# A never-taken branch behind another wait, a residual as one matrix product, and the order of the store's two waits, in a one-core decode kernel

## The chip, the cores and the metric

The kernel runs on one core of a Trainium2 chip. A core has five engines that run their own instruction streams and meet only through semaphores: TensorE (PE in the profile; PEld is its weight loads), VectorE (DVE), ScalarE (ACT), GpSimd (POOL) and SyncE (SP), which issues the transfers. Sixteen DMA engines carry data between the device memory and the on-chip memory. The metric is the device time of one execution in microseconds. For the kernel before, three runs gave 190.36, 190.53 and 191.09 us, so the median is 190.53 us.

## What is computed

One token goes through an attention block over a long cache and then through a small MLP block. Cut to what matters:

```python
def _A_ref(x, k_cache, v_cache, wq, wo):           # 32 query heads, 8 cached heads, 16384 positions
    q = (x @ wq) as heads of 128
    p = softmax(q . k * 128 ** -0.5)
    return (p . v) @ wo

def _B_ref(x, w1, w2, w3, w4):                     # S = 1
    h  = gelu(layernorm(x) @ w1)
    hs = shifted(h) @ w2                           # shifts along a sequence of length 1
    x1 = x + hs
    return x1 + gelu(layernorm(x1) @ w3) @ w4      # w3: 512 x 1792, w4: 1792 x 512

h  = x + _A_ref(layernorm(x), ...)
h2 = h + _B_ref(layernorm(h), ...)
```

For one position the four shifted quarters of `h` are all zero, so `hs` is zero and `w1` and `w2` have no part in the output; the kernel doesn't load them. What is left of the second block is two normalizations, the product with w3, gelu, the product with w4 and the residual sums.

## The kernel before

The weights and the cache are read once, some 79 MB, by SyncE's transfers in the order of the program: wq, then keys and values of four pairs of cached heads, then wo in three pieces (`WO`), w3 in two (`W3`) and w4 in four (`W4`, cut at rows 5, 10 and 13 of 14 steps). Keys go alternately into two halves of `kb`, values into `vb`; wo later takes the first half of `kb`, and w3 and w4 take the second. A transfer into a buffer waits until its readers are done.

TensorE runs the four pairs in a loop with register waits (`_tensor`, lines 154 to 316): scores from transposed keys (L600), softmax pieces, the product with the values (L636), a gather (L658). Behind the loop stands straight-line code, which is what the change is about: the product with wo (L702), a sum over rows (L708), the statistics of the normalization (L493), the product with w3 (L720), the residual (L738) and the product with w4 (L746).

The layout of the tail: the 512 outputs stand as four blocks of 128 columns in four groups of 32 partitions of the bank `n_ps`. `BLOCK = (0, 2, 1, 3)` says which block stands in which group. The residual L738 is four products, one per group; each takes 32 columns of the fp32 identity `ident_f` as weights and `xsum` (128x128, fp32) as the moving matrix, and opens the accumulation. L746 adds to it, in 14 steps `m` of four products each. Step `m` needs the piece of w4 that holds its rows and the half of `hcol` that holds its column: steps 0 to 6 need `("hcol", 0)`, steps 7 to 13 `("hcol", 1)`. `hcol` is the transposed gelu: ScalarE makes gelu in two halves `hg` (L729), VectorE transposes each (L733).

A recording layer, `Program`, keeps for each engine the list of operations with the operations they depend on. `_wants` turns these into one wait per semaphore, and `_run` puts the waits ahead of the instruction, unless an earlier wait of the same engine covered them. An operation whose function is `None` marks the place of a branch: on TensorE `pe(None)` (L744) stands ahead of step `W4[-2][0]`, which is 10; on VectorE `dve(None)` (L736) stands behind the transposes. There `_tensor` and `_vector` emit a comparison that is never true, with a jump back to early code and a hint for it:

```python
self._run(eng, ops[hi:on], seen)
eng.br_lt(rl, 0, "pe_pair", "pe_on").branch_hint(hint)
nc.switch_bb("pe_on", parent=None)
self._run(eng, ops[on + 1:], seen)
```

What the marker depends on is not looked at: L314 emits no wait of its own.

At the end ScalarE (L751) and VectorE (L753) copy a half each of the result into `fin`, and SyncE stores it (L754), waiting for both, then waits for the store (L756). The first of its two waits in the program is carried by the store itself, the other by an instruction of its own ahead of it.

GpSimd makes the identity at the start (L520), fills `qb` and `pt` with zeros (L534, L535), computes two small powers (L509) and tells TensorE that values have landed.

Of the kernel before, what the change touches and what calls it, by code (L numbers as in the profile page):

```python
# [6 lines left out]
FP32 = mybir.dt.float32  # L7
# [17 lines left out]
class Program:  # L25
# [128 lines left out]
    def _tensor(self):  # L154
        nc, eng, ops = self.nc, self.nc.tensor, self.ops["PE"]
# [40 lines left out]
        for o in loop:  # L196
            a = o.at
            v = waits.get((a[0], last, *a[2:]))
# [14 lines left out]
        sem, v0, _ = told[0, 0]  # L213
# [4 lines left out]
        r, rl, ry, rq, rk = (eng.alloc_register(n) for n in ("seen", "landed", "half", "query", "piece"))  # L218
# [3 lines left out]
        seen = {}  # L222
# [87 lines left out]
        seen[id(sem)] = told[last, parts - 1][2]  # L310
        on = next(n for n, o in enumerate(ops) if o.fn is None)
        self._run(eng, ops[hi:on], seen)

        eng.br_lt(rl, 0, "pe_pair", "pe_on").branch_hint(hint)  # L314
        nc.switch_bb("pe_on", parent=None)
        self._run(eng, ops[on + 1:], seen)
# [15 lines left out]
W4 = ((0, 5), (5, 10), (10, 13), (13, 14))  # L332
BLOCK = (0, 2, 1, 3)
# [9 lines left out]
def bass_sequential_preLN__gqa_block_cached__mixer_s_mlp__decode_kernel(  # L343
# [13 lines left out]
    with ExitStack() as ctx:  # L357
        sb = lambda name, shape, dt: ctx.enter_context(nc.sbuf_tensor(name, shape, dt))
# [13 lines left out]


        x4 = sb("x4", [4, 128], BF16)
        mean4 = sb("mean4", [128, 128], FP32)
        ident_f = sb("ident_f", [128, 128], FP32)
        ident = sb("ident", [4, 4], BF16)
# [34 lines left out]
        xsum = sb("xsum", [128, 128], FP32)  # L412
        hg = sb("hg", [128, FQ], BF16)
        hT = sb("hT", [128, NCH, 32], FP32)
        hcol = sb("hcol", [128, NHC, 32], BF16)
        fin = sb("fin", [64, 256], BF16)
# [13 lines left out]
        m_ps, n_ps = mn_ps[:, 0:256], mn_ps[:, 256:512]  # L430
# [28 lines left out]
        def dve(fn, r=(), w=(), bank=()):  # L459
            return P.op("DVE", fn, r, w, bank)  # L460
# [4 lines left out]
        def pool(fn, r=(), w=(), bank=()):  # L465
            return P.op("POOL", fn, r, w, bank)

        def pe(fn, r=(), w=(), bank=(), also=()):

            return P.op("PE", fn, r, w, bank, also=also)  # L470

        def piece(cuts, m):
            return [lo <= m < hi for lo, hi in cuts].index(True)
# [23 lines left out]
        def variance(i):  # L497
# [7 lines left out]
            for n in range(1 + i):  # L505
# [22 lines left out]
            r=["ident", "x4"], w=["quarter"])  # L528
        pe(lambda e: e.matmul(O_ps[0][:, 0:128], quarter[:, :, :].rearrange("p q u -> p (q u)"), x4[:, :],
                              start=True, stop=True), r=["quarter"], w=[("O", 0)], bank=[("O", 0)])  # L530
# [2 lines left out]
        act(lambda e: e.activation(scr[0:1, 0:1], mean4[0:1, 0:1], ACTF.Exp), r=["mean4"], w=["scr"])  # L533
        pool(lambda e: e.memset(qb[:, :, :, :], 0.0), w=["qb"])  # L534
        pool(lambda e: e.memset(pt[:, :, :, :, :], 0.0), w=["pt"])  # L535

        dve(lambda e: e.tensor_reduce(row32[:, :], ident_f[:, :].rearrange("p (c r) -> p r c", c=4), AX.X, ALU.add),
            r=["ident_f"], w=["row32"])
        dve(lambda e: e.tensor_reduce(maskdd[:, :], ident_f[:, :].rearrange("p (n d) -> p d n", d=4), AX.X, ALU.add),
            r=["ident_f"], w=["maskdd"])  # L540
# [6 lines left out]
        for z, m, key, mk in ((zo, rowgh, "zo", "rowgh"), (zd, maskgh, "zd", "maskgh")):  # L547
# [5 lines left out]
            r=["hT", (("st", 0), 0), (("st", 0), 6)] + [("v", x) for x in range(VP)], w=["xn"])  # L553
# [3 lines left out]
        for i, key in enumerate(keys):  # L557
            P.part("query", i)
            for k in range(NCH):
                pe(lambda e, k=k: e.matmul(row[:, bass.ds(P.b, 512)], copies(xn[:, k:k + 1], 128),  # L560
                                           wq_k[:, k, bass.ds(P.c, REP * DH)], start=(k == 0), stop=(k == NCH - 1)),
                   r=["xn"], also=[("v", x) for x in range(VP)], w=["n" if key == "mn" else key], bank=[key])
        P.part()
        for g in range(2):
            half = banks[64 * g:64 * g + 64, PAIRS * g:PAIRS * g + PAIRS, :].rearrange("p j c -> p (j c)")
            for b in range(2):
# [3 lines left out]
                    r=["n" if x == "mn" else x for x in keys[PAIRS * g:PAIRS * g + PAIRS]], w=["qcol"],  # L570
                    bank=keys[PAIRS * g:PAIRS * g + PAIRS])
# [120 lines left out]
        for n, (lo, hi) in enumerate(W4):  # L692
# [4 lines left out]
            r=["o_m"], w=["o_f"])  # L697
        dve(lambda e: e.tensor_copy(o_b[:, :], o_f[:, :]), r=["o_f"], w=["o_b"])

        for r_ in range(32):  # L700
# [3 lines left out]
               r=["o_b", ("r", 0, piece(WO, r_))], w=[("O", 0)], bank=[("O", 0)])  # L704
        h_ps, hkey = banks[:, 6, :], "spare0"
        dve(lambda e: e.tensor_copy(osum[:, :], O_ps[0][:, :]), r=[("O", 0)], w=["osum"], bank=[("O", 0)])  # L706
        for q in range(4):
            pe(lambda e, q=q: e.matmul(h_ps[32 * q:32 * q + 32, 0:128], copies(row32[:, 0:1], 32),  # L708
                                       osum[:, q * 128:(q + 1) * 128], start=True, stop=True),
               r=["osum", "row32"], w=[hkey], bank=[hkey])  # L710
        s = st[1]
# [3 lines left out]
            r=["hT", (S, 0)] + [("r", 1, 0)], w=["hc"])  # L715


        for k in range(NCH):
            for q in range(4):
                pe(lambda e, k=k, q=q: e.matmul(s_ps[32 * q:32 * q + 32, 0, 0:FQ], hc[:, k, :],  # L720
                                                w3_sb[:, k, q * FQ:(q + 1) * FQ], start=(k == 0), stop=(k == NCH - 1)),
                   r=["hc"] + [("r", 1, n) for n in (piece(W3, k),) if n], w=[("s", 0)], bank=[("s", 0)])
# [3 lines left out]
            r=["hr", "xs", (S, 6)], w=["xsum"])  # L726
# [7 lines left out]
                hcol[:, lo:hi, :].rearrange("p m u -> p (m u)"),  # L734
                hg[:, :].rearrange("p (i m) -> p m i", m=NHC)[:, lo:hi, :]), r=[("hg", n)], w=[("hcol", n)])
        dve(None)  # L736
        for o in range(4):
            pe(lambda e, o=o: e.matmul(  # L738
                n_ps[32 * o:32 * o + 32, 0:128], ident_f[:, 32 * BLOCK[o]:32 * BLOCK[o] + 32], xsum[:, :],
                start=True, stop=False, skip_group_check=True),  # L740
               r=["ident_f", "xsum"], w=["n"], bank=["mn"])
        for m in range(NHC):
            if m == W4[-2][0]:
                pe(None)  # L744
            for o in range(4):
                pe(lambda e, m=m, o=o: e.matmul(  # L746
                    n_ps[32 * o:32 * o + 32, 0:128], hcol[:, m, :], w4_sb[:, m, BLOCK[o] * 128:(BLOCK[o] + 1) * 128],
                    start=False, stop=(m == NHC - 1),
                    skip_group_check=True),
                   r=[("hcol", 2 * m // NHC), ("r", 1, len(W3) + piece(W4, m))], w=["n"], bank=["mn"])  # L750
        act(lambda e: e.activation(fin[:, 0:128], n_ps[0:64, 0:128], ACTF.Identity),  # L751
            r=["n"], w=[("fin", 0)], bank=["mn"])
        dve(lambda e: e.tensor_copy(fin[:, 128:256], n_ps[64:128, 0:128]), r=["n"], w=[("fin", 1)])  # L753
        P.op("SP", lambda e: e.dma_start(out[0, 0:1, :].rearrange("o (q j) -> (o q) j", q=2), fin[31:33, :]),  # L754
             r=[("fin", 0), ("fin", 1)], w=["out"], dma="out")
        P.op("SP", lambda e: e.nop(), r=["out"])  # L756
        P.emit()

# [29 lines left out]
```

## Time and profile before

| what | value |
|---|---|
| median of three runs | 190.53 us |
| the profiled execution's own time | 190.37 us |
| its span, first to last instruction | 188.84 us |
| mean granted TensorE clock | 0.82 |
| read from device memory | 79.17 MB, 419 GB/s over the span |
| busy: PE, DVE, ACT, POOL | 62%, 61%, 5%, 3% |
| store issued, span ends | 187.69 us, 188.84 us |

The profile is of one execution. Times in it are microseconds from the start of the span, and L12 is line 12 of the kernel. The time of a run is longer than the span, since it also has what stands ahead of the first and behind the last instruction. A row of the timeline merges neighbouring instructions of a kind: start, length, engine, line, operation, output<-inputs, shapes, their count, and in brackets how long the engine had been idle before it and what released it. A "q" behind an engine's name means its sequencer: waits, branches and the issue of transfers. The chain of waits follows the work that ended last back from the end, at each step to what released it.

### The profile page before, as it was taken

Reading aid. Unit: us, or ns where it says so; the run is one execution under the profiler, and the core shown is the slowest. Engines: PE = TensorE matmul, PEld = TensorE weight load, DVE = VectorE, ACT = ScalarE, POOL = GpSimd, SP = SyncE. Lnnn points to the kernel's source line nnn. Section 1 sums busy time; section 2 is a strip of 40 time slices with the busy share of each in tenths; the row PEclk is TensorE's granted clock in tenths of the full one; section 3 lists DMA queues with packets and bytes.
Section 4 is the critical chain, followed back from the end, with each engine's and each line's share of the span. In section 5 each row is a group of like instructions: output and inputs, shape, how many; then the busy total and the mean of one; then the engine's idle time right before and its main releaser. Section 6 shows DMA issues by size and latency. Waiting matters only on the chain.

```text
span 188.8 us, 2175 instructions
## 1 busy us (share of the span) xinstructions
PE 116.5 (62%) x701; PEld 45.5 (24%) x701; DVE 115.4 (61%) x140; ACT 9.3 (5%) x16; POOL 5.7 (3%) x10
## 2 busy tenths in 40 slices
PE   1009908998174499950732999616739996192754
PEld 1003303433031134320310333202213332030222
DVE  4900599995524999945047989550279897514052
ACT  3000000000200000002000000020000000500011
POOL 1900000000000000000000000000000000000010
PEclk9999965999759669996596699965766999669685
DMA  6999999999799999898999999999999999989994
GB/s 222 444 444 444 444 423 465 444 444 444 333 444 444 444 555 416 389 430 347 423 437 444 444 444 444 444 444 396 403 423 444 444 444 444 430 380 423 415 408 168
DMA packets 3325, 79.19 MB, mean 419 GB/s; under 512 B 378, under 2 KB 508, under 8 KB 1276
## 3 DMA queue, kind: packets, MB, share of 16 engines
q1 hardware_dynamic: 3316, 79.17, 97.8%
q8 instruction: 1, 0.02, 0.0%
q10 hardware_dynamic: 8, 0.00, 0.0%
HBM read 79.17 MB, written 0.00 MB: 419 GB/s over the span
## 4 chain that ended last, share of the span: by engine, by line
DMA 66%; DVE 17%; PE 9%; issue 6%; SPq 1%; DVEq 0%
DMA kb<-in_A_k_cache_dram 45%; DVE kt L583 15%; DMA kb<-in_B_w_dram 14%; DMA vb<-in_A_wq_dram 7%; PE banks L560 5%; PE banks L600 4%; SPq L434 1%; DVE qcol L567 1%; DVE qb L574 0%; PE banks L746 0%; PE banks L594 0%; DVE xn L551 0%; DVE fin L753 0%; SPq L137 0%; DVEq L137 0%
## 5 line engine op out<-in xcount | busy, mean ns | idle before, releaser
L583 DVE STREAM_TRANSPOSE kt<-kb 128x2048 int32<-128x2048 int32 (+1 forms) x37 | 71.3, 1989 | 5.6 <-DMA kb<-in_A_k_cache_dram 4.0
L600 PE MATMUL banks<-kt,qn 128*128 x256 | 69.4, 416 | 0.4
L600 PEld LDWEIGHTS banks<-kt,qn 128*128 x256 | 26.3, 103 | 41.9 <-issue 26.2
L636 PE MATMUL banks<-vb,pt 128*32 128x512 bf16 x256 | 21.3, 505 | 2.9 <-POOLq L449 2.9
L652 DVE TENSOR_SCALAR od<-banks,rowc 128x128 f32<-128x128 f32 x4 | 1.4, 350 | 23.3 <-PE banks L636 23.3
L560 PE MATMUL banks<-vb,xn 128*128 x32 | 9.4, 467 | 9.8 <-DVE xn L551 9.8
L594 PE MATMUL banks<-qn 128*128 128x512 bf16 x8 | 4.0, 496 | 18.1 <-DVE kt L583 17.8
L625 DVE STREAM_TRANSPOSE pt<-p_sb 64x1024 bf16<-64x1024 bf16 x8 | 9.9, 1239 | 5.4 <-ACT p_sb L621 5.3
L621 ACT ACTIVATE p_sb<-banks,bias 128x1024 bf16<-128x1024 f32 x4 | 4.5, 1114 | 155.5 <-DVE nmh L617 155.5
L643 PE MATMUL banks<-acc,zd 128*32 128x1 f32 x8 | 1.1, 202 | 17.7 <-DVE pt L625 17.7
L636 PEld LDWEIGHTS banks<-vb,pt 128*32 128x32 bf16 x256 | 8.0, 123 | 14.3 <-issue 8.5
L610 DVE TENSOR_REDUCE mx<-banks 128x1 f32<-128x1024 f32 x4 | 4.9, 1224 | 8.1 <-PE banks L600 8.1
L567 DVE STREAM_TRANSPOSE qcol<-banks 64x1024 f32<-64x1024 f32 x4 | 4.8, 1227 | 7.5 <-PE banks L560 7.5
L560 PEld LDWEIGHTS banks<-vb,xn 128*128 128x128 bf16 x32 | 3.7, 116 | 15.1 <-issue 12.8
L509 POOL TENSOR_TENSOR st<-st,expo 128x1 f32<-128x1 f32 (+1 forms) x2 | 1.3, 630 | 176.2 <-DVE st L507 176.2
L613 PE MATMUL banks<-mxd,mean 128*128 128x128 f32 x8 | 2.0, 326 | 6.6 <-DVE mxd L611 6.6
L594 PEld LDWEIGHTS banks<-qn 128*128 128x128 bf16 x8 | 0.8, 100 | 20.9 <-issue 20.8
L658 PE MATMUL banks<-od,zo 128*32 128x128 f32 x8 | 1.6, 285 | 6.5 <-DVE od L655 6.5
L702 PE MATMUL banks<-kb,o_b 128*32 128x512 bf16 x32 | 3.5, 621 | 2.8 <-DMA kb<-in_A_wo_dram 2.8
L643 PEld LDWEIGHTS banks<-acc,zd 128*32 128x32 f32 x8 | 0.7, 140 | 18.4 <-DVE pt L625 18.4
L655 DVE SCALAR_TENSOR_TENSOR od<-banks,rowc,od 128x128 f32<-128x128 f32 x12 | 4.2, 351 | 0.4
L706 DVE COPY osum<-banks 128x512 f32<-128x512 f32 x1 | 0.7, 692 | 5.3 <-PE banks L702 5.3
(71 smaller groups left out, 45.2 us busy)
## 6 DMA issues: line engine op xcount, KB each, us to landing
kb<-in_A_k_cache_dram SPq DMA_DIRECT2D x8, 4096.0 KB, 29.7
vb<-in_A_v_cache_dram SPq DMA_DIRECT2D x2, 4096.0 KB, 29.0
vb<-in_A_wq_dram SPq DMA_DIRECT2D x1, 4096.0 KB, 12.3
kb<-in_A_wo_dram SPq DMA_DIRECT2D x1, 3072.0 KB, 27.4
kb<-in_B_w_dram SPq DMA_DIRECT2D x1, 1344.0 KB, 23.3
kb<-in_B_w_dram SPq DMA_DIRECT2D x2, 640.0 KB, 25.7
kb<-in_A_wo_dram SPq DMA_DIRECT2D x1, 768.0 KB, 28.9
kb<-in_B_w_dram SPq DMA_DIRECT2D x1, 448.0 KB, 24.1
```

Source lines behind the costliest of these rows:

```text
L560: pe(lambda e, k=k: e.matmul(row[:, bass.ds(P.b, 512)], copies(xn[:, k:k + 1], 128), wq_k[:, k, bass.ds(P.c, REP * DH)], start=(k == 0), s ...
L567: dve(lambda e, g=g, b=b, half=half: e.transpose(qcol[64 * g:64 * g + 64, 2 * b:2 * b + 2, :, :].rearrange("p e m u -> p (e m u)"), half.r ...
L583: P.op("DVE", lambda e, view=view: e.transpose(view(kt), view(kb[y])), r=[("r", y, i) for i in range(RPARTS)], w=[("kt", t + i) for i in r ...
L594: pe(lambda e: e.matmul(row[:, bass.ds(P.y, 512)], copies(none, 128), copies(none, 512), start=True, stop=False, skip_group_check=True), r ...
L600: pe(lambda e, n=n: e.matmul(row[:, bass.ds(P.y, 512)], qn[:, n, bass.ds(P.q, 128)], key_piece(P.k, n), start=False, stop=(n == 3), skip_g ...
L610: dve(lambda e: e.tensor_reduce(mx[:, :], s_all, AX.X, ALU.max), r=[("s", 0), ("s", 1)], w=["mx"], **both)
L613: pe(lambda e: e.matmul(m_ps[:, 0:128], mean4[:, :], mxd[:, :], start=True, stop=True), r=["mxd", "mean4"], w=["m"], bank=["mn"])
L621: act(lambda e: e.activation(p_sb[:, :], s_all, ACTF.Exp, bias=bias[:, 0:1], scale=float(SCALE), accum_out=acc[:, :]), r=[("s", 0), ("s", ...
L625: dve(lambda e, g=g: e.transpose(pt[64 * g:64 * g + 64, :, :, g, :], p_sb[64 * g:64 * g + 64, :]), r=["p"], w=["pt"])
L636: pe(lambda e, l=l, ct=ct, ch=ch: e.matmul(O_ps[0][32 * ct:32 * ct + 32, :], pt[:, l, ch, :, :].rearrange("p g u -> p (g u)"), tiles[:, l ...
L655: dve(lambda e, block=block, c=c: e.scalar_tensor_tensor(od[:, :], block, rowc[:, c:c + 1], od[:, :], ALU.mult, ALU.add), r=[key, "rowc", ...
L702: pe(lambda e, r_=r_, q=q: e.matmul(O_ps[0][32 * q:32 * q + 32, :], copies(o_b[:, r_:r_ + 1], 32), wo_sb[:, r_ * D:(r_ + 1) * D], start=(r ...
```

## The change

It has three edits.

1. The marker `pe(None)` moves from step 10 (`W4[-2][0]`) to step 5 (`W4[0][1]`) and now reads `("hcol", 1)`; `_tensor` emits the waits of the marker ahead of the branch and notes them, so that step 7 needs no wait for the same half any more.
2. The four residual products with 32 columns of the identity each become one product with a 128x128 matrix `swapped`: the identity with its two middle blocks of 32 columns exchanged. GpSimd makes it once at the start, behind the two fills. `swapped` is a new tile of 512 bytes per partition, allocated behind `x4`.
3. The store names the half from VectorE ahead of the one from ScalarE, so that the wait it carries itself is the one for VectorE.

```diff
@@ -310,7 +310,10 @@
         on = next(n for n, o in enumerate(ops) if o.fn is None)
         self._run(eng, ops[hi:on], seen)
-
+        for i, (s, v, _) in self._wants(ops[on]).items():
+            if seen.get(i, 0) < v:
+                eng.wait_ge(s, v)
+                seen[i] = v
         eng.br_lt(rl, 0, "pe_pair", "pe_on").branch_hint(hint)
...
         x4 = sb("x4", [4, 128], BF16)
+        swapped = sb("swapped", [128, 128], FP32)
...
         pool(lambda e: e.memset(pt[:, :, :, :, :], 0.0), w=["pt"])
+        pool(lambda e: e.tensor_copy(swapped[:, :].rearrange("p (b a c) -> p b a c", a=2, b=2),
+                                     ident_f[:, :].rearrange("p (a b c) -> p b a c", a=2, b=2)),
+             r=["ident_f"], w=["swapped"])
...
         dve(None)
-        for o in range(4):
-            pe(lambda e, o=o: e.matmul(
-                n_ps[32 * o:32 * o + 32, 0:128], ident_f[:, 32 * BLOCK[o]:32 * BLOCK[o] + 32], xsum[:, :],
-                start=True, stop=False, skip_group_check=True),
-               r=["ident_f", "xsum"], w=["n"], bank=["mn"])
+        pe(lambda e: e.matmul(
+            n_ps[:, 0:128], swapped[:, :], xsum[:, :], start=True, stop=False, skip_group_check=True),
+           r=["swapped", "xsum"], w=["n"], bank=["mn"])
         for m in range(NHC):
-            if m == W4[-2][0]:
-                pe(None)
+            if m == W4[0][1]:
+                pe(None, r=[("hcol", 1)])
...
         P.op("SP", lambda e: e.dma_start(out[0, 0:1, :].rearrange("o (q j) -> (o q) j", q=2), fin[31:33, :]),
-             r=[("fin", 0), ("fin", 1)], w=["out"], dma="out")
+             r=[("fin", 1), ("fin", 0)], w=["out"], dma="out")
```

On TensorE the program of the tail is then: one residual product, the 20 products of steps 0 to 4, the wait for the second half of `hcol` with the branch, the 36 products of steps 5 to 13, each w4 piece still waited for at its first step. VectorE, ScalarE and the order of SyncE's transfers are as before; GpSimd has one instruction more.

## The prediction

> **What bounds the kernel now.** I read the page first: the span, the DMA row, the share of the queues and the chain.
>
> ```profile
> span 188.8 us, 2175 instructions
> DMA  6999999999799999898999999999999999989994
> q1 hardware_dynamic: 3316, 79.17, 97.8%
> DMA 66%; DVE 17%; PE 9%; issue 6%; SPq 1%; DVEq 0%
> ```
>
> The DMA engines are busy nine tenths or more of almost every slice, the one bulk queue fills 97.8% of their time, and two thirds of the chain is transfer. The kernel streams 79 MB. All three edits sit in the last 5 us or in the first 10, so the next view is the end of the chain (start us, length us, what):
>
> ```profile
> 159.79 26.82 DMA kb<-in_B_w_dram
> 186.61 0.04 issue
> 186.65 0.65 PE banks L746 x12
> 187.29 0.02 issue
> 187.32 0.29 DVE fin L753
> ```
>
> The transfer issued at 159.79 lands at 186.61, and TensorE starts 0.04 us later. Length 26.82 identifies it: of the w4 pieces, the 384 KB one has a median of 26.8 us to landing.
>
> ```profile
> kb<-in_B_w_dram SPq DMA_DIRECT2D x1, 384.0 KB, 26.8
> ```
>
> That is the third of four pieces, rows 10 to 12 of the fourteen steps `m`. Then the timeline of the last microseconds (start us, length us, engine, line, names, idle before and its releaser):
>
> ```profile
> 183.31 0.35 DVE L725 SCALAR_TENSOR_TENSOR xsum<-xs,st,hr 128x128 f32<-128x128 f32 x1 [0.70 <-POOL st L509]
> 183.78 0.23 PEld L738 LDWEIGHTS banks<-xsum,ident_f 128*32 128x32 f32 x8 [0.80 <-POOL st L509]
> 183.81 0.66 PE L738 MATMUL banks<-xsum,ident_f 128*32 128x128 f32 x8
> 184.35 1.04 DVE L733 STREAM_TRANSPOSE hcol<-hg 128x224 bf16<-128x224 bf16 x2 [0.69 <-ACT hg L729]
> 184.98 1.39 PE L746 MATMUL banks<-kb,hcol 128*32 128x128 bf16 x40 [0.52 <-DVE hcol L733]
> 185.65 0.46 PEld L746 LDWEIGHTS banks<-kb,hcol 128*32 128x32 bf16 x20 [0.21 <-DMA kb<-in_B_w_dram]
> 186.65 0.39 PEld L746 LDWEIGHTS banks<-kb,hcol 128*32 128x32 bf16 x16 [0.55 <-DMA kb<-in_B_w_dram]
> 186.65 0.62 PE L746 MATMUL banks<-kb,hcol 128*32 128x128 bf16 x16 [0.28 <-DMA kb<-in_B_w_dram]
> 187.32 0.27 ACT L751 ACTIVATE fin<-banks 64x128 bf16<-64x128 f32 x1 [2.64 <-PE banks L746]
> 187.32 0.29 DVE L753 CAST fin<-banks 64x128 bf16<-64x128 f32 x1 [1.93 <-PE banks L746]
> 187.69 0.33 SPq L754 DMA_DIRECT2D out_dram<-fin  x1
> ```
>
> The last product is fed piece by piece. Steps 0 to 4 start when the first half of `hcol` is there (184.98). Steps 5 to 9 wait for the second w4 piece, which by the 0.04 us of the chain landed at 185.61. Steps 10 to 13 wait for the third. Between 186.37 (184.98 + 1.39) and 186.65 TensorE has nothing to do. So the end is set by the landing of weights, not by gelu, transposes or residual.
>
> **The change part by part.** *The branch.* It and the packet of code that TensorE or another engine fetches near the end are seen in these rows: the two never-taken branches (ns min/median/max, then start us), and windows of the tail, whose last two columns are the DMA share and GB/s.
>
> ```profile
> L314 PEldq COMPARE_BRANCH  x1: 73/73/73, 185.7 to 185.7; - x1
> L150 DVEq COMPARE_BRANCH  x1: 67/67/67, 184.7 to 184.7; - x1
> q8 instruction: 1, 0.02, 3.9%
> 186.20:186.40 0.20, 0.17 (x8) 0.00 (x0) 0.00 (x0) 0.00 (x0) 0.00 (x0) 0.50 0.28 97
> 186.40:186.45 0.05, 0.00 (x0) 0.00 (x0) 0.00 (x0) 0.00 (x0) 0.00 (x0) 0.50 0.02 0
> 186.45:186.75 0.30, 0.10 (x8) 0.10 (x12) 0.00 (x0) 0.00 (x0) 0.00 (x0) 0.50 0.00 0
> 186.75:186.80 0.05, 0.05 (x8) 0.05 (x11) 0.00 (x0) 0.00 (x0) 0.00 (x0) 0.50 1.18 328
> ```
>
> TensorE's branch takes 73 ns, now ahead of step 10. After the change it stands ahead of step 5 and first waits for the second half of `hcol`. The two transposes end at 184.35 + 1.04 = 185.39; with the same 0.04 us the branch starts at 185.43 and ends at 185.50. Step 5 can't start before 185.61 anyway, so wait and branch lie under the second piece's landing with 0.11 us to spare. Behind the new wait stand 36 matmuls, and behind those the two `fin` copies and the store. Had the transposes been later, the first 0.11 us would be free, and another 0.28 us would be taken by TensorE's idle time before 186.65; beyond 0.39 us it would cost one for one. The old in-line wait of step 7 for the same `hcol` half disappears, having been satisfied since 185.39. Cost: 0, cover 0.11 us and then 0.28 us.
>
> *What the branch may move.* The q8 row was asked for from 186.47 to 188.00: one code packet, 0.02 MB, 3.9% of 16 engines over 1.53 us, which is 0.95 us of one engine (1.18 x 0.05 x 16 = 0.94 from the window). It starts between 186.75 and 186.80. TensorE's branch starts at 185.7, so 185.65 to 185.75, and ends by 185.72 to 185.82: the packet follows by 0.93 to 1.08 us. VectorE's branch is 2 us earlier, which is further; the nearer one is the likelier trigger, but nothing shows it. If TensorE's it is, the packet moves to 186.43 to 186.58 (185.50 plus that delay). The w4 packets are over by 186.45: the windows show 97 GB/s to 186.40, a 0.02 share without bytes to speak of to 186.45, and nothing after. So it would start at the very end of the weights or just behind them. Its price lies between 0 and 0.94 us, the length of the packet if a w4 packet of the same engine stood behind it; below nothing it could reach -0.3 us (the shift, 185.7 to 185.43) if the end of the program waits for this code. I take 0, because nearly all of 186.43 to 186.58 is clear.
>
> The Trainium skill, "Runtime: NRT & Kernel Launch", section "Instruction fetch mechanics", says that a sequencer refills its instruction memory in 16 KiB blocks and fetches the next while it runs the current one, strictly in sequence, and that only a taken branch out of the window stalls. By this a branch that is never taken starts no fetch, wherever it stands, and the time would be my 190.50 with nothing left for the first two rivals below. The trace agrees on the size (328 GB/s in 0.05 us is 16.4 KB); that the packet comes 1 us behind a branch speaks rather the other way, so I keep both rivals.
>
> *The residual.* Four products of 32 columns (8 passes, 183.81 to 184.47) become one of 128 columns, which I expect in two passes as each of the four had. No row has it here, but these two have its parts: a weight load of 128x128 fp32 in this stage, and fp32 products of 128x128 by 128x128.
>
> ```profile
> 181.14 0.30 PEld L493 LDWEIGHTS banks<-rs,mean 128*128 128x128 f32 x2 [1.02 <-DVE xs L489]
> L613 PE MATMUL banks<-mxd,mean 128*128 128x128 f32 x8 | 2.0, 326 | 6.6 <-DVE mxd L611 6.6
> ```
>
> At most 0.30 + 2 x 0.33 = 0.96 us one after the other, so it ends by 183.78 + 0.96 = 184.74; at least 0.33 us if all overlaps, 184.11. `hcol` releases TensorE at 184.98. Cost and gain both 0; the cover is 0.24 us at worst, and without it the excess would first eat the waits named above.
>
> *The swapped identity.* One more GpSimd copy at the start, behind the two memsets:
>
> ```profile
> 1.54 0.29 POOL L520 TENSOR_SCALAR_AFFINE_SELECT ident_f<-ident_f 128x128 f32<-128x128 f32 x1 [1.10 <-DVE ident_f L519]
> 5.51 2.18 POOL L534 MEMSET qb<- 128x2496 bf16 x1
> 7.62 1.80 POOL L535 MEMSET pt<- 128x2048 bf16 x1
> 5.83 3.63 DVE L548 COPY zo<-rowgh 128x32 f32<-128x32 f32 x1
> 13.12 0.29 DVE L551 TENSOR_SCALAR xn<-hT,st 128x4 bf16<-128x4 f32 x1 [3.64 <-DMA vb<-in_A_wq_dram]
> ```
>
> The nearest row is the same shape on GpSimd, 0.29 us; the far bound is the longest GpSimd row, 2.18 us. VectorE's small copy of `zo` is stretched to 9.46, just when GpSimd's memsets end (9.42), so the copy may hold VectorE by its own length too. VectorE then waits until 13.12 for wq. 9.46 + 2.18 = 11.64 is still in front of that: cost 0, cover 3.64 us. Behind it on GpSimd stand only waits for the values, which land later still, and the second power function at the end. The new tile also moves every later tile by 512 bytes; no row prices this, and the transfers keep their sizes, so I take 0.
>
> *The store.* SP waits for both halves of `fin`; the order of the two waits changes.
>
> ```profile
> L137 SPq EVENT_SEMAPHORE  x1: 17/17/17, 187.6 to 187.6; - x1
> ```
>
> Now the separate wait instruction (17 ns) is for VectorE, which ends last (187.32 + 0.29 = 187.61 against ScalarE's 187.59), and the store issues at 187.69. Afterwards that instruction waits for ScalarE and is done while VectorE finishes. The gain lies between nothing and the whole 0.08 us from 187.61 to 187.69; one wait instruction and a step to the next, 0.03 us, is my value.
>
> *The sum.* -0.03 us and otherwise 0. The profiled execution took 190.37 us, 1.53 more than its span as 188.84; it becomes 190.34. It lies 0.16 under the median of the runs, 190.53, which becomes 190.50.
>
> **The rivals.** A difference under 0.5%, 0.95 us, is about what a measurement of this kernel can't tell from no change.
>
> First, *the code packet meets the last w4 packets*. It needs a start some 0.05 us or more earlier than I have it, on the engine that is last. For it: the lower end, 186.43, touches the weights. Against: most of the range is clear. It delays the last piece, on which four matmuls and the end wait: 0.47 us on the mean of 0 and 0.94, so 191.0; at most 191.4, which is 0.49%.
>
> Second, slower: *the code behind the branch isn't there*. The branch stood before 16 matmuls and now stands before 36; if it falls through into code that must be fetched first, TensorE stands until branch end + delay + packet, 185.50 + 1.0 + 0.94 = 187.44. Then 36 matmuls: 20 took 0.72 us (185.65 to 186.37) and 16 took 0.62, so four cost 0.10 and 36 cost 1.12, and they end at 188.56 instead of 187.27: +1.29 us, 191.8, or 0.7%. It decides as soon as a fetch ends later than 186.6. Against: before, twelve matmuls behind the branch ran at 186.65, ahead of any code packet, so their code was there, and that of steps 5 to 9 was as well. The Trainium skill, "Runtime: NRT & Kernel Launch", section "Instruction fetch mechanics", has such a stall for a taken branch; no trace here shows one.
>
> Third, *the end waits for the code*: a packet 0.3 us earlier makes the program's end earlier by as much, 190.2. For: 1.53 us of the run lie outside the span. Against: the packet ends at 187.7, the store is only issued then, and the span ends 1.1 us later.
>
> That the branch changes nothing because another engine's code is in that packet is a fourth, with 190.50 as well.
>
> **How the numbers follow.** No change at 190.50, the fourth case included: 0.66. The packet meets the weights: 0.12, a third of it beyond 0.5% with the scatter of runs (0.04). Code missing: 0.09, slower. The end earlier: 0.06, inside the bound. A gain beyond it that I can't name: 0.07. So slower 0.13, faster 0.07, within 0.80. The range goes down to the third rival less the 0.17 us from the lowest run to the median, 190.0, and up to the first rival's far bound, 191.4; the second rival, the first's worst and the unnamed gain are left out, 0.20.
>
> **What would show it.** Right: steps 5 to 9 and 10 to 13 start 0.04 us behind their pieces' landings, the branch starts at about 185.43 and lies in the wait, the code packet shifted by 0.3 us, the residual over before `hcol`, the store some 0.05 us behind VectorE. Wrong: a gap on TensorE behind the branch with a code packet in it (second rival), a last piece that lands late with code beside it (first), a shorter time outside the span (third), or wq's product starting later than 13.1 us.

## The result, and the profile after

The changed kernel takes 190.17 us (median of 20 runs, 189.92 to 190.65), the kernel before 190.47 (20 runs, 190.28 to 191.09). The ratio is 0.9981, 95% interval 0.9973 to 0.9989: a gain of 0.36 us, between 0.21 and 0.51. That is inside the 0.5% that the prediction called no change, but larger than the 0.03 us of its sum, and the interval leaves out 1.

The page of the changed kernel first, then the end of its chain (start us, length us, what):

```profile
span 188.9 us, 2164 instructions
DMA  6999999999799999997999999997999999999994
q1 hardware_dynamic: 3316, 79.17, 98.0%
DMA 66%; DVE 18%; PE 10%; issue 4%; SPq 1%; DVEq 0%
```

```profile
159.94 26.79 DMA kb<-in_B_w_dram
186.73 0.04 issue
186.77 0.65 PE banks L751 x15
187.42 0.02 issue
187.44 0.29 DVE fin L758
```

Nothing has moved in the chain: the third w4 piece lands and TensorE starts 0.04 us later, as before. There are 12 TensorE instructions less and one on GpSimd more (2164 against 2175). The profiled execution's span is 188.94 us, 0.10 longer than the one before, because in this execution w4 landed 0.12 us later. Yet the execution took 190.25 us, where the one before took 190.37. So in this execution the gain isn't in the span. The tail of the timeline, the branch's row (ns min/median/max, start), and windows around the code packet (last two columns DMA share and GB/s):

```profile
183.70 0.50 PEld L744 LDWEIGHTS banks<-xsum,swapped 128*128 128x128 f32 x2 [0.73 <-POOL st L513]
183.70 0.80 PE L744 MATMUL banks<-xsum,swapped 128*128 128x128 f32 x2
184.34 1.05 DVE L740 STREAM_TRANSPOSE hcol<-hg 128x224 bf16<-128x224 bf16 x2 [0.80 <-ACT hg L736]
184.98 1.53 PE L751 MATMUL banks<-kb,hcol 128*32 128x128 bf16 x40 [0.48 <-DVE hcol L740]
185.78 0.45 PEld L751 LDWEIGHTS banks<-kb,hcol 128*32 128x32 bf16 x20 [0.35 <-DMA kb<-in_B_w_dram]
186.77 0.62 PE L751 MATMUL banks<-kb,hcol 128*32 128x128 bf16 x16 [0.27 <-DMA kb<-in_B_w_dram]
187.44 0.29 DVE L758 CAST fin<-banks 64x128 bf16<-64x128 f32 x1 [2.05 <-PE banks L751]
187.79 0.33 SPq L759 DMA_DIRECT2D out_dram<-fin  x1
```

```profile
L317 PEldq COMPARE_BRANCH  x1: 73/73/73, 185.4 to 185.4; - x1
```

```profile
186.45:186.60 0.15, 0.06 (x4) 0.00 (x0) 0.00 (x0) 0.00 (x0) 0.00 (x0) 0.50 0.24 82
186.60:186.65 0.05, 0.00 (x0) 0.00 (x0) 0.00 (x0) 0.00 (x0) 0.00 (x0) 0.50 1.48 328
186.65:188.40 1.75, 0.62 (x16) 0.36 (x16) 0.29 (x1) 0.27 (x1) 0.00 (x0) 0.50 0.00 0
```

The branch starts at 185.4 and the second w4 piece is awaited until 185.78. The residual is over at 184.50, ahead of 184.98. The code packet starts between 186.60 and 186.65, some 0.15 us earlier than before, and the last w4 packets started less than 0.2 us ahead of it. The store issues 0.06 us behind VectorE's copy (187.73 to 187.79), where it was 0.08.

The runs tell where the gain lies: each has its time and its span. Outside the span the changed kernel has 1.35 us on the mean of 20 runs, with a standard deviation of 0.05. The kernel before has 1.71 us with 0.2, between 1.41 and 2.32, in the 87 runs that stood beside the experiments; of its 20 runs above, no spans are on record. The spans are alike, 188.88 and 188.83 us. One run of e10 below, 197.51 us with a span of 194.5 us at a granted clock of 0.69, was in a slower state of the chip and is left out of e10's figures.

### The profile page after: what moved, and what is told of

Its sections match the earlier page's. It is cut to its first block, busy times and chain, and to the rows that moved or that the text cites. A ratio compares the mean times of both kernels' runs of the same rounds, so it can differ in the third digit from the quotient of the medians.

```text
span 188.9 us, 2164 instructions
## 1 busy us (share of the span) xinstructions
PE 117.9 (62%) x695; PEld 46.2 (24%) x695; DVE 115.3 (61%) x140; ACT 9.3 (5%) x16; POOL 5.9 (3%) x11
## 4 chain that ended last, share of the span: by engine, by line
DMA 66%; DVE 18%; PE 10%; issue 4%; SPq 1%; DVEq 0%
DMA kb<-in_A_k_cache_dram 45%; DVE kt L590 16%; DMA kb<-in_B_w_dram 14%; DMA vb<-in_A_wq_dram 6%; PE banks L567 5%; PE banks L607 5%; SPq L438 1%; DVE qcol L574 1%; DVE qb L581 0%; PE banks L751 0%; PE banks L601 0%; DVE xn L558 0%; DVE fin L758 0%; SPq L137 0%; DVEq L137 0%
## 5 line engine op out<-in xcount | busy, mean ns | idle before, releaser
L607 PE MATMUL banks<-kt,qn 128*128 x256 | 68.5, 411 | 0.5
L643 PE MATMUL banks<-vb,pt 128*32 128x512 bf16 x256 | 23.9, 555 | 3.0 <-POOLq L453 3.0
L643 PEld LDWEIGHTS banks<-vb,pt 128*32 128x32 bf16 x256 | 8.8, 134 | 16.3 <-issue 11.9
L555 DVE COPY zo<-rowgh 128x32 f32<-128x32 f32 x1 | 3.6, 3630 | 0.0
```

The source lines that it names most:

```text
L555: dve(lambda e, z=z, m=m: e.tensor_copy(z[:, :].rearrange("p (n d) -> p n d", d=4), m[:, :, :].rearrange("p g h -> p (g h)").unsqueeze(2). ...
L607: pe(lambda e, n=n: e.matmul(row[:, bass.ds(P.y, 512)], qn[:, n, bass.ds(P.q, 128)], key_piece(P.k, n), start=False, stop=(n == 3), skip_g ...
L643: pe(lambda e, l=l, ct=ct, ch=ch: e.matmul(O_ps[0][32 * ct:32 * ct + 32, :], pt[:, l, ch, :, :].rearrange("p g u -> p (g u)"), tiles[:, l ...
```

## Experiments

All ratios are against the kernel before, run beside it on the same chip; they are the record's own figures and not quotients of two medians. The deviations are of the time outside the span.

| kernel | median us | ratio, 95% interval | span, mean | outside, mean (deviation) |
|---|---|---|---|---|
| e1 before again | 190.39 | 0.9995 (0.9985 to 1.0005) | 188.83 | 1.63 (0.10) |
| e2 branch only | 190.40 | 0.9991 (0.9981 to 1.0001) | 188.83 | 1.66 (0.22) |
| e3 residual only | 190.19 | 0.9980 (0.9970 to 0.9990) | 188.85 | 1.35 (0.05) |
| e4 store only | 190.63 | 1.0005 (0.9992 to 1.0017) | 188.80 | 1.86 (0.24) |
| e5 12 instructions more | 190.41 | 0.9996 (0.9985 to 1.0006) | 188.84 | 1.67 (0.24) |
| e6 6 instructions more | 190.30 | 0.9989 (0.9980 to 0.9998) | 188.78 | 1.48 (0.08) |
| e7 copy only | 190.46 | 1.0001 (0.9993 to 1.0010) | 188.81 | 1.71 (0.12) |
| e8 no branch | 191.40 | 1.0050 (1.0034 to 1.0066) | 190.10 | 1.33 (0.04) |
| e9 no wait | 190.13 | 0.9978 (0.9969 to 0.9987) | 188.78 | 1.32 (0.06) |
| e10 long code, late branch | 193.61 | 1.0132 (1.0090 to 1.0173) | 188.82 | 4.39 (1.10) |
| e11 short code, late branch | 190.17 | 0.9989 (0.9978 to 1.0001) | 188.79 | 1.45 (0.28) |
| e12 64 instructions more | 193.07 | 1.0131 (1.0112 to 1.0150) | 191.45 | 1.58 (0.02) |

### Which edit

The first four kernels take the change apart. e1 is the kernel before without any edit.

> The kernel before, unchanged, for the split of each run into its span and what lies outside it. The profiled execution had 1.53 us outside its span, the changed kernel's runs have 1.35 on their mean. If the gain of 0.3 us lies outside the span, this kernel's runs have 1.5 to 1.6 there; if it lies inside, they have 1.35 and a span 0.3 us longer than the changed kernel's. Ratio 1.000, within 0.001.

It had 1.63 us outside its span, a little more than expected, and a span of 188.83. So the gain of the change is outside the span. The runs of the kernel before that stood beside the experiments had 1.76 us outside beside e1 to e4, 1.69 beside e5 to e8 and 1.67 beside e9 to e12. As e1 is the same program and has 0.13 less than the runs beside it, a difference of 0.1 us between means of so wide a spread tells nothing.

e2 is the first edit alone, the move of the branch with its wait:

```diff
-            if m == W4[-2][0]:
-                pe(None)
+            if m == W4[0][1]:
+                pe(None, r=[("hcol", 1)])
```

> The moved branch with its wait alone; residual and store as before. Theory A (the program's end waits for something that the earlier branch starts, the prediction's third rival): the whole gain outside the span comes from here, outside 1.3 to 1.4 us, time -0.2 us against before. Theory B (TensorE's code is 12 instructions shorter): nothing, 1.5 to 1.6 us outside the span. Theory C (order of the store's waits): nothing.

1.66 us outside, ratio 0.9991 with 1 inside the interval: theory A's 1.3 to 1.4 us outside are not there. A smaller gain isn't excluded: the interval reaches down to 0.9981, and 0.10 us less outside than the runs beside it is what e1 shows without any edit.

e3 is the second edit alone, the residual as one product with the GpSimd copy and the tile:

```diff
-        for o in range(4):
-            pe(lambda e, o=o: e.matmul(
-                n_ps[32 * o:32 * o + 32, 0:128], ident_f[:, 32 * BLOCK[o]:32 * BLOCK[o] + 32], xsum[:, :],
...
+        pe(lambda e: e.matmul(
+            n_ps[:, 0:128], swapped[:, :], xsum[:, :], start=True, stop=False, skip_group_check=True),
+           r=["swapped", "xsum"], w=["n"], bank=["mn"])
```

> The residual as one product alone, with the new GpSimd copy and tile. Theory A: nothing, time within 0.05 us of before, 1.5 to 1.6 us outside the span. Theory B: 1.3 to 1.4 us outside the span, time -0.2 us. In the tail the product ends by 184.7 us, ahead of the release of the last product, in either theory.

1.35 us outside with a deviation of 0.05, ratio 0.9980: the whole gain, and the spread is gone as well. Theory B's numbers.

e4 is the third edit alone:

```diff
-             r=[("fin", 0), ("fin", 1)], w=["out"], dma="out")
+             r=[("fin", 1), ("fin", 0)], w=["out"], dma="out")
```

> The order of the store's two waits alone. Theories A and B: a store that issues 0.02 to 0.05 us sooner behind VectorE's copy, time -0.03 us, which a measurement hardly tells. Theory C: most of the gain, -0.2 to -0.3 us.

Ratio 1.0005: no gain that can be told. Theory C falls.

### What in the residual

The residual edit does three things: less work in the tail, 12 instructions less in TensorE's program, and a copy on GpSimd with a tile that moves the others. e5 and e6 keep the tail of the change and lengthen the program elsewhere, by repeating its first small product at 2 us, which writes the same values again. e5 has it 7 times in all, e6 4 times:

```diff
-        pe(lambda e: e.matmul(O_ps[0][:, 0:128], quarter[:, :, :].rearrange("p q u -> p (q u)"), x4[:, :],
-                              start=True, stop=True), r=["quarter"], w=[("O", 0)], bank=[("O", 0)])
+        for _ in range(7):
+            pe(lambda e: e.matmul(O_ps[0][:, 0:128], quarter[:, :, :].rearrange("p q u -> p (q u)"), x4[:, :],
+                                  start=True, stop=True), r=["quarter"], w=[("O", 0)], bank=[("O", 0)])
```

> The changed kernel with its first product repeated six times, at 2 us: 12 TensorE instructions more, so its program is as long as before, while the tail is that of the change. Theory L (the length or position of TensorE's code decides what the end costs): 1.6 to 1.8 us outside the span as before, time back to 190.4 to 190.6. Theory W (the 12 instructions less in the tail itself): 1.35 outside, time as the change, 190.2. The repeats cost at most 0.6 us at 2 us and are hidden by the wait for wq until 13.1 us.

> The same with three repeats, 6 TensorE instructions more than the change. Theory L with a threshold: either 1.35 or 1.6 to 1.8 us outside the span, nothing between; theory L with a gradual cost: 1.5. Theory W: 1.35.

With 12 instructions more, the time outside the span is back at 1.67 us with the wide spread (1.40 to 2.16), and the gain is gone. With 6 more it is 1.48, between. The tail is that of the change in both, so theory W falls. The length of TensorE's program decides. That it does so gradually is not shown: e6's twelve runs lie in two groups, five from 1.36 to 1.42 us and seven from 1.53 to 1.58, as far as spans on record to 0.1 us can tell.

e7 keeps the copy and the tile, but the four products; the copy is read by nobody.

```diff
+        swapped = sb("swapped", [128, 128], FP32)
...
+        pool(lambda e: e.tensor_copy(swapped[:, :].rearrange("p (b a c) -> p b a c", a=2, b=2),
+                                     ident_f[:, :].rearrange("p (a b c) -> p b a c", a=2, b=2)),
+             r=["ident_f"], w=["swapped"])
```

> Before, with the GpSimd copy and the new tile but the four residual products kept; the copy is then read by nobody. Theory G (the copy or the moved tiles made the gain): 1.35 us outside the span. Theories L and W: 1.6 to 1.8, time as before.

1.71 us outside, ratio 1.0001: theory G falls. Copy and moved tiles cost nothing that can be told.

### What the branch does

e8 takes hint and branch, and the marker's wait with them, out of the changed kernel's TensorE program.

```diff
-        hint = eng.mark_branch_hint_location()
...
-        eng.br_lt(rl, 0, "pe_pair", "pe_on").branch_hint(hint)
-        nc.switch_bb("pe_on", parent=None)
```

> The changed kernel without TensorE's hint and never-taken branch, two instructions fewer. If the branch starts the one code packet of the tail, the packet of 0.02 MB is gone from its place near 186.7 us, and stands earlier, where it can hold back a weight transfer (0 to +0.9 us), or nowhere; time 190.2 to 191.1. If another engine's branch starts it, it stays at 186.6 to 187.3 and the time is 190.2.

The kernel becomes 0.5% slower than before, all of it in the span (190.10), with the short 1.33 us outside. In the DMA view of its tail, from 174 to 190 us, there is no code packet; in the 0.02 us from 101.87 there is (the second row is the one of its queue):

```profile
DMA packets 1, 0.02 MB, mean 819 GB/s; under 512 B 0, under 2 KB 0, under 8 KB 0
q8 instruction: 1, 0.02, 334.1%
```

334.1% of 16 engines over 0.02 us is 1.07 us of one engine, in the middle of the stream. Its chain then goes through wo:

```profile
149.29 27.42 DMA kb<-in_A_wo_dram
176.71 0.14 issue
176.85 3.63 PE banks L700 x25
```

In the changed kernel the same product has this row:

```profile
175.77 3.27 PE L709 MATMUL banks<-kb,o_b 128*32 128x512 bf16 x32 [1.32 <-DMA kb<-in_A_wo_dram]
```

TensorE begins it at 176.85 instead of 175.77, 1.1 us later, about the packet's length. The trace's records of landings show what the packet held back. Each bulk transfer lands in sixteen parts. In the changed kernel the last part comes at most 0.14 us behind the one before it, in every transfer. In e8 it comes at most 0.05 us behind until 100.2 us, and 1.2 to 1.3 us behind in each of the 15 transfers that land later than the packet. That fits one of the sixteen DMA engines held back by the packet for the rest of the run, though the record doesn't name the engine. So the packet is TensorE's code, and hint and branch together keep it out of the stream; which of the two does, no run separates.

e9 keeps the change's branch and drops its wait.

```diff
-                pe(None, r=[("hcol", 1)])
+                pe(None)
```

> The changed kernel with the branch ahead of step 5 but without its wait for hcol: it follows the issue of step 4, at 185.1 instead of 185.4. If the packet follows TensorE's branch by 1 to 1.7 us, it starts at 186.1 to 186.8, part of the time among the last w4 packets, which are over by 186.45; then the last two landings and the span grow by 0 to 0.9 us, on the mean 0.1 to 0.4, with a wider spread of the spans than the change's 0.19 us. If w4 is never met, the span stays at 188.8 to 188.9, and the wait is worth nothing; 1.35 us outside the span either way.

In its profile the branch came at 184.2, and the packet started in the first of these windows, while w4 was still moving:

```profile
185.90:185.95 0.05, 0.05 (x16) 0.05 (x8) 0.00 (x0) 0.00 (x0) 0.00 (x0) 0.50 2.17 615
185.95:186.45 0.50, 0.42 (x16) 0.15 (x8) 0.00 (x0) 0.00 (x0) 0.00 (x0) 0.50 0.34 115
186.45:187.00 0.55, 0.38 (x16) 0.30 (x16) 0.00 (x0) 0.00 (x0) 0.00 (x0) 0.50 0.00 0
```

Nevertheless the last products ran as usual. The last of the sixteen parts of each later w4 piece landed 0.07 us behind the one before it, where the transfers ahead of the packet had 0.04 to 0.08, so in this execution the packet held none of them back. The spans are 188.78 us with a deviation of 0.10: the wait is worth nothing in these runs.

### Whether the end waits for the packet

e10 and e11 put the branch ahead of step 13, e10 in the long program of before:

```diff
-            if m == W4[-2][0]:
+            if m == W4[-1][0]:
```

> Before, with the branch ahead of step 13 instead of 10, so about 0.9 us later; the long code. If the end of a long program waits for the code packet, the packet now ends near 188.7 to 189 and the time outside the span grows from 1.7 to 2.2 to 2.8 us, time +0.5 to +1.0 us. If the long code costs a fixed time that has nothing to do with the packet, it stays at 1.6 to 1.8. Span unchanged, as the branch's 73 ns lie ahead of the last piece's landing.

and e11 in the short one of the change:

```diff
-            if m == W4[0][1]:
+            if m == W4[-1][0]:
                 pe(None, r=[("hcol", 1)])
```

> The changed kernel with the branch ahead of step 13 instead of 5, so about 1.3 us later; the short code. If the short program's end doesn't need the packet, 1.35 us outside the span and 190.2, although the packet ends near 189. If it does, 1.8 us or more outside.

The long program lost 2.7 us on the mean outside its span (4.39 in five runs, from 2.49 to 5.36, against 1.67 beside it), more than expected: in its profile, of the run with the most, no code packet is seen between 186.6 and 188.7, and it comes at 190.69, behind the span. The short one stays at a median of 1.34 us, though its packet is on its way when the store is, as its branch's row and this window show; one of its 12 runs had 2.27.

```profile
L317 PEldq COMPARE_BRANCH  x1: 77/77/77, 186.7 to 186.7; - x1
187.75:187.80 0.05, 0.00 (x0) 0.00 (x0) 0.00 (x0) 0.00 (x0) 0.00 (x0) 0.50 1.73 328
```

So the end of the long program needs the packet and the end of the short one does not, as a rule.

The trace also records the updates of the semaphores. Behind the span the engines meet (a few updates of semaphore 2), and then each sets its share of the semaphores back. The share 7 to 53 is the last to start and the only one that moves with TensorE's program, so I take it for TensorE's. From these records, one execution each, in us:

```
program           code packet ends,     share 7-53 starts,    share 7-53 starts,
                  after the meeting     after the meeting     after the packet's end
before (long)         -1.39                 0.46                  1.85
e1 (long)             -1.31                 0.50                  1.81
e2 (long)             -1.18                 0.56                  1.74
e4 (long)             -0.83                 0.69                  1.52
e5 (long)             -0.55                 1.10                  1.65
e7 (long)             -1.20                 0.54                  1.75
e10 (long)            +2.60                 4.24                  1.65
e6 (half)             -1.16                 0.22                  1.38
after (short)         -1.41                 0.22                  1.63
e3 (short)            -0.78                 0.22                  0.99
e9 (short)            -2.04                 0.32                  2.36
e11 (short)           +0.03                 0.22                  0.19
e12 (64 more)         -4.13                 0.22                  4.35
```

In long programs the start follows the packet's end by 1.5 to 1.9 us, wherever that is. In short ones it stands at 0.22 to 0.32 us after the meeting, and where the packet is makes no difference. e6's traced execution, one of its lower group, starts like a short one, and its last recorded update comes 1.26 us after the meeting, where the change has 1.15.

### Where the edge lies

e12 is e5 with the first product 33 times in all, in place of 7:

```diff
-        for _ in range(7):
+        for _ in range(33):
```

> The changed kernel with its first product repeated 32 times: 64 TensorE instructions more than the change. If a block of code ends just behind the program, as theory L with a threshold has it, its edge now falls among the last steps of the w4 product, behind the branch, in a block that is fetched only after the branch: TensorE stands in the tail for the packet, a gap of 1 to 2 us among steps 6 to 10, span 189.8 to 191 (the prediction's second rival). If theory L is no matter of a block's edge, the span stays at 188.8 to 189.0 and 1.6 to 1.8 us lie outside it. The repeats end by 6 us, ahead of wq's landing at 13.1 us.

The span grew to 191.45 us. This is TensorE's timeline in e12:

```profile
185.00 1.16 PE L752 MATMUL banks<-kb,hcol 128*32 128x128 bf16 x31 [0.38 <-DVE hcol L741]
189.18 0.91 PE L752 MATMUL banks<-kb,hcol 128*32 128x128 bf16 x25 [3.02 <-issue]
```

and its windows around the code packet:

```profile
186.50:186.55 0.05, 0.00 (x0) 0.00 (x0) 0.00 (x0) 0.00 (x0) 0.00 (x0) 0.50 1.54 328
186.55:187.50 0.95, 0.00 (x0) 0.00 (x0) 0.00 (x0) 0.00 (x0) 0.00 (x0) 0.50 0.00 0
```

After 31 of the 56 products TensorE stands for 3.02 us and waits for nothing that the profile shows ("issue"); the packet takes 1.54 x 0.05 x 16 = 1.23 us from about 186.5, and TensorE goes on 1.4 us after its end. That is the prediction's second rival. It costs 3.02 us less the 0.28 us of idle time that was there anyway, 2.7; the spans grew by 2.6. It also places the edge: behind the stop come 25 products and 24 weight loads, 49 instructions. In a program that is 64 longer than the change's, the block ends 49 ahead of the program's end; in the change's own it ends 15 behind it, in e6 9 behind, in before and e5 3 behind. Those few instructions are the closing code ahead of the semaphores' reset: which of them the next block holds is inferred, since the profile doesn't list them. e12 also shows that the edge counts and not the length: its program is the longest, yet TensorE's share starts 0.22 us after the meeting as in the short ones, as by this working the packet had brought all of its closing code. Why e12 also has 1.58 us outside its span, and not 1.35, stays open; its last recorded update comes 1.15 us after the meeting, as in the change, so the difference isn't among these records.

## Why the prediction was right, and where it was not

*No change beyond 0.5%, time near 190.5.* Right: 190.17, 0.19% less.

*The branch costs nothing, with 0.11 us to spare.* Right. It starts at 185.4 and the matmuls start 0.04 us behind the landings.

*The packet follows TensorE's branch.* Right, and now shown: without hint and branch it moves to 101.9 us (e8). Its start was said to be 186.43 to 186.58 and was 186.60 to 186.65; the delay behind the branch's end was 1.1 us or a little more. As a fixed delay it was too narrow: the other traces with the branch have 1.0 to 1.1 us but for e9 with 1.6, e6 with 1.7 and e10 with 4.0, and no run shows why.

The Trainium skill, "Runtime: NRT & Kernel Launch", section "Instruction fetch mechanics", has the next page fetched in sequence while the current one runs. e8 agrees: left alone, the packet comes in mid-stream. A branch that is never taken has no part in that rule, and here the measurement differs: hinted, it held the packet back until it ran, and code behind it was waited for (3.02 us in e12) though no jump was taken. That only a taken branch stalls, as the prediction has it, this section of the Trainium skill doesn't state: it names that stall and no other.

*First rival, the packet meets w4.* In the change it comes just behind them. Where it starts while they still move (e9), it held none of them back and the span doesn't grow, so no run shows the price of 0.47 us. What a packet costs with transfers behind it on its engine, e8 shows: the last part lands 1.2 to 1.3 us late, more than the 0.94 that was taken as the most.

*Second rival, code that isn't there.* The mechanism exists. It did not decide here because the program ends 15 instructions ahead of the edge, by the working from e12. Its price was too small: 1.29 us by my sum, 2.6 in e12, as TensorE goes on only 1.4 us after the packet's end and not at once.

*Third rival, the end waits for the code.* Its place and size are the measured ones, outside the span and 190.2, but it hung on the wrong edit. In the long program the end does follow the packet (the table above), but the moved branch alone (e2) gave nothing that stands clear of no change. Whether it moved the packet by 0.3 us there isn't shown: in e2's one traced execution, its slowest, the packet ended 1.18 us ahead of the meeting, where it was 1.39 before and 1.31 in e1. What removes the wait is the shorter program, after which the end doesn't need the packet.

*The residual, "cost and gain both 0".* This is the term that was mis-sized. As work it is 0, as said: it ended at 184.50, within the bounds 184.11 to 184.74, under the wait for `hcol`. But its 12 instructions of code are worth 0.38 us (e3, 0.9980 of 190.6; 0.19 to 0.57 by its interval), outside the span, where the sum looked only through the branch. That the total still fell into the stated range is owed to its lower bound, 190.0, which came from the third rival, and not to this term. The rows before held a hint: 1.53 us outside the span and a code packet ending 1.1 us ahead of the span's end, which I read as time enough.

*The GpSimd copy, cost 0.* Right: 0.29 us as its bound's near row said. VectorE's copies ended with the memsets and not with it.

```profile
9.38 0.29 POOL L540 COPY swapped<-ident_f 128x128 f32<-128x128 f32 x1
5.84 3.63 DVE L555 COPY zo<-rowgh 128x32 f32<-128x32 f32 x1
```

These two rows of the changed kernel's timeline have VectorE's copy end at 9.47 and GpSimd's copy run from 9.38 to 9.67.

*The store, -0.03 us.* The step behind VectorE shrank by about 0.02 us in the profile; no run can tell it (e4).

## What to carry to other kernels

An instruction that is hidden as work can still cost as code: count an edit's instructions on each engine, and compare time and span of the runs, since a gain or loss outside the span shows in no row of the timeline. A code packet took 0.93 to 1.40 us in these traces, and in e8 it held one sixteenth of every later transfer back by 1.2 to 1.3 us, so in a kernel bound by transfers it matters when it is fetched, and the code behind its edge must not be needed until well over 1 us after it has landed. Of this change one edit carries the gain; with the residual alone, or with the wait dropped, the kernel is as fast (ratios 0.9980 and 0.9978 against 0.9981).

## What the hardware showed that was not expected

TensorE goes on only 1.4 us (e12) to 1.9 us (before) after the end of the packet that it needs. A branch that is placed too late makes things worse than its delay: 0.9 us later (e10) put the packet 3.9 us later, at 190.7 us, in the one execution that was traced; why, no run shows. And the time outside the span of one and the same kernel varied from 1.41 to 2.32 us with the long code of before, and from 1.28 to 1.46 with the short code of the change.
